# Decay rows spread by DMA into the probability tiles, and layer 1's gate scale and bias applied at its output

## The chip, the cores and the metric

One Trainium2 chip, of which the program uses one core. The metric is device time in microseconds (us). The kernel before took 1080.01 us in the median of three runs (1076.92 to 1083.23). "PE" is the matmul engine (TensorE) and "PEld" its weight loads, "DVE" is VectorE, "ACT" ScalarE, "POOL" GpSimd, "SP" SyncE, which issues nearly all DMAs.

## The reference

Forget attention, then two MLPs, all in float32 outputs (the MLP weights arrive as float64 and are split on the chip).

```python
def _attn_ref(q, k, v, s):                # q, k, v: 4 x 8 x 576 x 64; s: 4 x 8 x 576
    scale = 1.0 / np.sqrt(D)
    scores = scale * np.matmul(q, k.transpose(0, 1, 3, 2))
    cum = np.cumsum(np.maximum(s, 0.0), axis=-1)
    bias = -(cum[:, :, :, None] - cum[:, :, None, :])
    scores = np.where(causal, -1000000000.0, scores + np.minimum(bias, 0.0))
    attn = np.exp(scores - np.max(scores, axis=-1, keepdims=True))
    attn = attn / (np.sum(attn, axis=-1, keepdims=True) + 1e-09)
    return np.matmul(attn, v)

def _moe_ref(x, w_in, w_out, s, b):       # x: 2304 x 512, w_in: 512 x 2048, w_out: 2048 x 512
    r = np.maximum(x @ w_in, 0.0)
    g = s * (r * r) + b                   # s and b are one number each
    return g @ w_out

def _moe2_ref(x, w_in, w_out, alpha):
    h = x @ w_in
    g = np.maximum(h, 0.0) + alpha * np.minimum(h, 0.0)
    return g @ w_out
```

The output of the attention, heads side by side, is the input of the first MLP, and its output the input of the second.

## The kernel before, in words

**Attention.** The work is cut into 32 units (`units`): a batch, a pair of heads, and a range of rows (range 0: rows 0 to 319 in blocks 0 to 2; range 1: rows 320 to 575 in blocks 3 and 4). `sum_gates` sums the gates along the sequence, writes the sums of all 32 heads to memory (`cum_d`, L98) and turns them into a column per block (`cumT`). `load_cum` spreads one head's row of sums over all 128 partitions by a DMA whose source row is repeated (tile `cum`, L263). `scores` then makes the decay of each block on DVE: row minus column, at most 0 (L339), into the block's part of the tile `probs`; POOL clears the padding (L335) and masks the upper triangle (L343). PE's scores are added on DVE with the row maximum (L365), ACT takes the exponential (L371), POOL divides by the sum (L380). `values` turns the probabilities on PE (L411, tile `pt`) and multiplies by v (L427). A head's scores run beside the head before's values; `probs` has two buffers. Units 1 to 3 use weight slots for their tiles.

**Layer 1.** Tokens go in blocks of 256, seven of them, and one block of 512 at the end ("the wide block", `count == 2`). `up` makes `hp` (L573) in a block of 128 hidden units f; ACT applies relu and square (L586, L587), POOL multiplies by the gate's scale and adds its bias (L588), and the result is split into two parts for exact products (L106 on ACT, L107 on POOL or DVE); `down` adds to `acc` (L599) two steps later (`LAG`). `finish` takes `acc` out of PSUM, half on DVE (L614), half on ACT (L612), and the next block's first products into the same banks wait for it. The weights of f (512 KB `wi` and 512 KB `wo`) come during the first block and are converted by ACT and DVE (L116 to L118); the buffers they land in (`RAW`) are few, so a load waits for a conversion.

**Layer 2.** During layer 1's wide block `fetch` and `prepare` bring the second layer's weights in eight pairs (wi and wo of f0 into `probs` buffers, those of f1 into `xh0` and `xl0`, which are free once the last 256-token block's `up` is through), convert them, form sums (L687 to L694), split them and write them to memory (`keep`, L683). `up2` (L763) and `down2` (L845) do the products.

**Order.** The instructions are written by Python generators that alternate attention with layer 1 at a pace set by `pace`; a scheduler then puts them into one fixed order on each engine. Each engine, and SP's list of DMAs, works strictly down its list.

## Time and profile before

| | |
|---|---|
| median of three runs | 1080.01 us |
| profiled execution, its own time | 1076.26 us |
| its span, first to last instruction | 1074.5 us |
| PE, PEld busy | 94%, 86% |
| DVE, ACT, POOL busy | 70%, 60%, 53% |
| mean granted PE clock | 0.978 of full |

A busy PE is one with a matmul under way by the profiler's model. Rows of a timeline give the start in us from the span's start, the duration, the engine, the line of the program, the tiles written and read, and in brackets the idle time before it with what ended it. A group's row gives the count behind an x, then busy time and the mean of one in ns.

### The profile page before, as it was taken

The numbers are of one execution on the slowest core, as the hardware profiler recorded it, in microseconds if no ns is written. First come the engines' busy times: TensorE is split into PE (matmuls) and PEld (weight loads), VectorE is DVE, ScalarE is ACT, GpSimd is POOL, SyncE is SP. The second block draws the span as 40 slices with busy tenths as digits, with TensorE's granted clock in tenths as the row PEclk, the third lists the DMA queues.
The fourth block names the chain that finished last, engine by engine and source line by source line (L and its number), as shares of the span: only waits on it lengthen the run. The fifth ranks groups of instructions, "written<-read, shape, count | busy, mean of one in ns | idle before, by whom it ended". The sixth has DMA issues, their size and how long they took to land.

```text
span 1074.5 us, 19671 instructions
## 1 busy us (share of the span) xinstructions
PE 1010.3 (94%) x6325; PEld 922.3 (86%) x6325; DVE 750.6 (70%) x1689; ACT 644.0 (60%) x1573; POOL 566.0 (53%) x987
## 2 busy tenths in 40 slices
PE   6799979989999999999999499699999999999998
PEld 4578869979999999999998478599899899999987
DVE  7789756687667666787651487897677566865665
ACT  3778557777777777868765376566354533543342
POOL 5444458877788677988774465542235211411121
PEclk9889999999999999999999789899999999999999
DMA  6897333343233332333331679998668565585511
GB/s 145 223 276 242 80 80 64 76 96 76 40 82 77 80 74 50 88 65 77 94 90 46 226 278 341 371 368 291 205 193 265 198 205 179 160 271 186 173 43 60
DMA packets 218216, 167.41 MB, mean 156 GB/s; under 512 B 140608, under 2 KB 164672, under 8 KB 218112
## 3 DMA queue, kind: packets, MB, share of 16 engines
q1 hardware_dynamic: 216432, 165.58, 51.7%
q8 instruction: 50, 0.82, 0.3%
q10 hardware_dynamic: 1680, 0.57, 0.2%
q14 instruction: 54, 0.44, 0.1%
HBM read 133.51 MB, written 32.58 MB: 155 GB/s over the span
## 4 chain that ended last, share of the span: by engine, by line
PE 70%; DVE 9%; DMA 6%; POOL 5%; ACT 4%; issue 3%; SPq 2%; DVEq 0%; POOLq 0%; ACTq 0%
PE d L845 19%; PE u L763 16%; PE hp L573 12%; PE acc L599 12%; PE av L427 4%; PE pt L411 4%; DMA wo<-in_moe_w_out_dram 2%; POOL r L588 2%; DVE probs L339 1%; PE sc L364 1%; PE sc L363 1%; DMA wi<-in_moe_w_in_dram 1%; PE sc L361 1%; SPq L240 1%; DVE probs L365 1%
## 5 line engine op out<-in xcount | busy, mean ns | idle before, releaser
L107 POOL TENSOR_TENSOR g<-r,g 128x256 fp32r<-128x256 f32 (+1 forms) x144 | 137.4, 954 | 274.0 <-ACT g L106 273.8
L573 PE MATMUL hp<-xh,w 128*128 128x256 f32 (+1 forms) x1024 | 231.4, 303 | 5.2 <-ACT r L586 3.6
L845 PE MATMUL d<-rw,g 128*128 128x512 f32 x864 | 211.3, 392 | 0.0
L599 PE MATMUL acc<-g,w 128*128 128x256 f32 x1344 | 200.6, 288 | 3.3 <-POOL g L107 1.9
L763 PE MATMUL u<-x,rw 128*128 128x384 f32 x1008 | 193.1, 340 | 9.4 <-ACT p L776 7.4
L763 PEld LDWEIGHTS u<-x,rw 128*128 128x128 f32 x1008 | 181.7, 191 | 16.7 <-ACT p L776 7.7
L845 PEld LDWEIGHTS d<-rw,g 128*128 128x128 f32 x864 | 161.1, 188 | 30.4
L573 PEld LDWEIGHTS hp<-xh,w 128*128 128x128 f32 x1024 | 173.1, 191 | 13.3 <-ACT r L586 5.3
L599 PEld LDWEIGHTS acc<-g,w 128*128 128x128 f32 x1344 | 176.1, 190 | 8.0 <-POOL g L107 2.7
L573 PE MATMUL hp<-xl,w 128*128 128x256 f32 (+1 forms) x512 | 152.8, 298 | 0.0
L106 ACT CAST g<-r 128x256 fp32r<-128x256 f32 (+1 forms) x208 | 94.3, 454 | 64.4 <-POOL r L588 29.4
L588 POOL TENSOR_SCALAR r<-r,gate_s,gate_b 128x256 f32<-128x256 f32 (+1 forms) x128 | 96.1, 751 | 49.5 <-ACT r L587 45.1
L380 POOL TENSOR_SCALAR probs<-probs,sm 64x64 f32<-64x64 f32 (+4 forms) x160 | 93.2, 594 | 36.2 <-DVE sm L377 30.3
L371 ACT ACTIVATE probs<-probs,nm 64x64 f32<-64x64 f32 (+4 forms) x160 | 89.9, 562 | 36.9 <-DVE nm L365 36.3
L853 DVE SCALAR_TENSOR_TENSOR sum<-d,sum 128x512 f32<-128x512 f32 x126 | 86.3, 686 | 33.9 <-PE d L845 33.7
L573 PEld LDWEIGHTS hp<-xl,w 128*128 128x128 f32 x512 | 98.0, 191 | 3.2 <-issue 0.7
L798 ACT ACTIVATE r<-u 128x384 f32<-128x384 f32 x72 | 36.7, 511 | 105.0 <-PE u L763 102.8
L365 DVE CUSTOM_DVE_ANT_0 probs<-sc,probs 128x320 f32<-128x320 f32 (+3 forms) x160 | 67.8, 426 | 43.8 <-PE sc L364 35.6
L411 PE MATMUL pt<-ident,probs 128*128 128x128 f32 x480 | 78.2, 284 | 13.7 <-POOL probs L380 13.6
L800 DVE SCALAR_TENSOR_TENSOR r<-v,nalpha,r 128x384 f32<-128x384 f32 x96 | 61.5, 643 | 31.0 <-ACT v L799 30.3
L411 PEld LDWEIGHTS pt<-ident,probs 128*128 128x128 f32 x480 | 56.9, 145 | 21.1 <-POOL probs L380 15.9
L339 DVE TENSOR_SCALAR probs<-cum,cumT 64x64 f32<-64x64 f32 (+4 forms) x160 | 66.1, 462 | 11.8 <-DMA cum<-cum_d 4.7
(141 smaller groups left out, 1763.1 us busy)
## 6 DMA issues: line engine op xcount, KB each, us to landing
rw<-wq SPq DMA_DIRECT2D x231, 256.0 KB, 4.1
wi<-in_moe_w_in_dram SPq DMA_DIRECT2D x32, 512.0 KB, 5.8
wo<-in_moe_w_out_dram SPq DMA_DIRECT2D x32, 512.0 KB, 5.7
cum<-cum_d SPq DMA_DIRECT2D x32, 288.0 KB, 3.6
wq<-rw SPq DMA_DIRECT2D x33, 256.0 KB, 6.0
wq<-q_xs SPq DMA_DIRECT2D x19, 256.0 KB, 5.4
cum<-cum_d SPq DMA_DIRECT2D x30, 160.0 KB, 3.1
nat<-in_k_dram SPq DMA_DIRECT2D x64, 72.0 KB, 2.4
```

The source lines that it names most:

```text
L106: nc.scalar.copy(hi, src)
L107: lo_eng.tensor_tensor(out=lo, in0=src, in1=hi.bitcast(F32), op=ALU.subtract)
L365: nc.vector.tensor_tensor_reduce(out=pt[:rows, j0:j1], in0=scr, in1=pt[:rows, j0:j1], scale=-SCALE, scalar=init, op0=ALU.add, op1=ALU.min, ...
L371: nc.scalar.activation(pt[:rows, :n], pt[:rows, :n], AF.Exp, bias=nm[:rows, m : m + 1], scale=-1.0, accum_out=sm[:rows, m : m + 1],)
L380: nc.gpsimd.tensor_scalar(out=probs[r][:rows, :n], in0=probs[r][:rows, :n], scalar1=sm[:rows, m : m + 1], scalar2=1.0, op0=ALU.mult, op1=A ...
L411: nc.tensor.transpose(tp[:, o : o + P], u.probs[h][r][:, k0 : k0 + P], ident)
L573: nc.tensor.matmul(hs, a[:, c], b[c], start=(n == 0), stop=(n == len(terms) * NCC - 1))
L588: nc.gpsimd.tensor_scalar(out=r, in0=r, scalar1=gate_s[:, 0:1], scalar2=gate_b[:, 0:1], op0=ALU.mult, op1=ALU.add)
L599: nc.tensor.matmul(banks[d] if count == 2 else acc[:, d], a[:, d * P : (d + 1) * P], b, start=(f == 0 and (d % 2 == 0 or count == 2) and n ...
L763: nc.tensor.matmul(dst, a[:, cols], b, start=(first and terms == 0), stop=(terms == 5), skip_group_check=True)
L845: nc.tensor.matmul(bank, a[:, cols], b, start=(terms == 0), stop=(terms == 5))
L853: nc.vector.scalar_tensor_tensor(out=total, in0=bank, scalar=1.0 / W_SCALE, in1=total, op0=ALU.mult, op1=ALU.add)
```

## The change

The rows of the decay no longer pass through DVE for every block. `sum_gates` makes, for all 32 heads at once, one row per block that is already relative to the block's first column, padded with zeros, five subtractions on 32 partitions in all, and writes them to two tensors in memory (768 and 1088 columns a head). `load_bias` spreads such a row over 128 partitions straight into the tile `probs`. What a row's own sum would have subtracted is the same for the whole row and falls out in the softmax. `probs` now has three buffers, the tiles `cum` are gone; sums and temporaries of layer 2 that used `cum` use `probs` and `res`. In layer 1, relu squared goes unscaled into the products; the scale is applied when `acc` leaves PSUM, with a bias of b times the column sums of `w_out`, which POOL adds up while the weights come (`colw`) and four one-column matmuls finish. The evictions of a 256-token block become four of 256 columns.

```diff
+    WIDE = [sum(-(-i1 // P) * P if i1 < S else S for _, i1 in IB[r]) for r in (slice(0, 3), slice(3, 5))]
+    bias_d = [dram.tile([B * H, n], F32, name=f"bias{z}_d") for z, n in enumerate(WIDE)]
...
-        nc.scalar.dma_start(out=cum_d, in_=cum)
-        for r, (i0, i1) in enumerate(IB):
-            n = i1 - i0
-            tp = ps.tile([P, 512], F32, tag="b", bufs=4, name=f"tp{r}")
-            nc.tensor.transpose(tp[:n, : B * H], cum[:, i0:i1], ident[: B * H, : B * H])
-            nc.vector.tensor_copy(cumT[:n, r, :], tp[:n, : B * H])
+        for z, blocks in enumerate((IB[:3], IB[3:])):
+            rows = two.tile([B * H, WIDE[z]], F32, tag="probs", name=f"bias{z}", bufs=3)
+            nc.gpsimd.memset(rows, 0.0)
+            col = 0
+            for i0, i1 in blocks:
+                nc.vector.tensor_scalar(
+                    out=rows[:, col : col + i1], in0=cum[:, :i1], scalar1=cum[:, i0 : i0 + 1], scalar2=None,
+                    op0=ALU.subtract,
+                )
+                col += -(-i1 // P) * P if i1 < S else S
+            nc.scalar.dma_start(out=bias_d[z], in_=rows)
...
+        if f == 0:
+            nc.gpsimd.tensor_scalar(out=colw, in0=values_[1], scalar1=1.0, scalar2=0.0, op0=ALU.mult, op1=ALU.add)
+        else:
+            nc.gpsimd.tensor_tensor(out=colw, in0=colw, in1=values_[1], op=ALU.add)
+        if f == NF - 1:
...
+                nc.tensor.matmul(
+                    total[:, d : d + 1], colw[:, d * P : (d + 1) * P], onecol, start=(d == 0), stop=(d == NCC - 1),
+                    skip_group_check=True,
+                )
...
-    def load_cum(u, heads=(0, 1)):
+    def load_bias(u, heads=(0, 1)):
...
+            row = bias_d[u.rng][u.b * H + u.h0 + h]
+            if u.early:
+                spans = ((0, 384), (384, 768))
...
+                whole = two.tile([P, 1088], F32, tag="probs", name=f"probs_{u.tag}_{h}", bufs=3)
...
+                (nc.sync if u.n else nc.scalar).dma_start(out=part, in_=row[c0:c1].partition_broadcast(P))
...
-            if width > i1:
-                nc.gpsimd.memset(pt[:, i1:], 0.0)
             if r == 0:
                 nc.gpsimd.memset(pt[64:P, 0:64], 0.0)
-
-            nc.vector.tensor_scalar(
-                out=pt[:rows, :i1], in0=u.cums[h][:rows, :i1], scalar1=cumT[:rows, r, head : head + 1],
-                scalar2=0.0, op0=ALU.subtract, op1=ALU.min,
-            )
...
             nc.scalar.square(r, r)
-            nc.gpsimd.tensor_scalar(
-                out=r, in0=r, scalar1=gate_s[:, 0:1], scalar2=gate_b[:, 0:1], op0=ALU.mult, op1=ALU.add
-            )
             split(gh, gl, r, nc.gpsimd if t and count == 1 else nc.vector)
...
+                    if d % 2:
+                        nc.scalar.activation(
+                            dst, src, AF.Identity, scale=gate_s[:, 0:1], bias=bsum[:, d : d + 1]
+                        )
+                    else:
+                        nc.vector.tensor_scalar(
+                            out=dst, in0=src, scalar1=gate_s[:, 0:1], scalar2=bsum[:, d : d + 1],
+                            op0=ALU.mult, op1=ALU.add,
+                        )
...
-        a1 = whole(two, "cum", S, "a1")
+        pair = two.tile([P, 1088], U32, tag="probs", name=f"a1_{p}", bufs=3)
+        a1 = pair[:, :512]
```

The scheduler puts the whole program anew. First, PE's list where the last 256-token block ends: `acc_6` is that block's output, `hp_n` the wide block's hidden units n, and `acc_7` the wide block's output, whose first products into the old banks wait for `acc_6` to be taken out. Before:

```order
L599 MATMUL acc_6_8113<-g_15_9042,w_15_2_62_1916 128x256 x2
L599 MATMUL acc_6_8113<-g_15_9042,w_15_2_61_1917 128x256
L599 MATMUL acc_6_8113<-g_15_9042,w_15_2_62_1916 128x256
L573 MATMUL hp_8_9627<-xh_1_8800,w_8_0_32_1272 128x512
L573 MATMUL hp_8_9627<-xl_1_8801,w_8_0_32_1272 128x512
L573 MATMUL hp_8_9627<-xh_1_8800,w_8_0_31_1273 128x512
L599 MATMUL acc_7_9061<-ring_9077,w_0_2_2_177 128x512
L599 MATMUL acc_7_9061<-ring_9077,w_0_2_1_178 128x512
```

And of the changed kernel, from the same last product of `acc_6` on:

```order
L617 MATMUL acc_6_7667<-g_15_8558,w_15_2_61_1817 128x256
L617 MATMUL acc_6_7667<-g_15_8558,w_15_2_62_1816 128x256
L594 MATMUL hp_5_8955<-xh_1_8322,w_5_0_19_1052 128x512
L594 MATMUL hp_5_8955<-xh_1_8322,w_5_0_20_1051 128x512
L594 MATMUL hp_5_8955<-xl_1_8323,w_5_0_20_1051 128x512
L594 MATMUL hp_5_8955<-xh_1_8322,w_5_0_19_1052 128x512
L594 MATMUL hp_6_8985<-xh_0_8320,w_6_0_24_1091 128x512
L594 MATMUL hp_6_8985<-xl_0_8321,w_6_0_24_1091 128x512
```

Before, three matmuls of 512 columns stand between the two; now the rest of `hp_5` and all of `hp_6` to `hp_8` stand there, 40 matmuls. Both lists have done `hp_0` to `hp_8` when they come to `acc_7`. Counted from the last product of `hp_15` of the last 256-token block (after which `xh0` and `xl0` are free), 27 matmuls of 512 columns and 24 of 256 precede that place before, and 63 and 24 now.

Second, SP's list of DMAs at the end of the attention, where layer 2's weights begin (`wi_n` and `wo_n` those of f = n, `wq` the memory that `keep` writes, `x_d` layer 1's output). Before:

```order
L143 DMA wi_0_8861<-in_moe_w_in_dram 128x4x256
L147 DMA wo_0_8862<-in_moe_w_out_dram 128x1024
L683 DMA wq_102<-q_0_xs_9123 128x512
L683 DMA wq_102<-q_0_xs_9124 128x512
L143 DMA wi_2_9114<-in_moe_w_in_dram 128x4x256
L147 DMA wo_2_9115<-in_moe_w_out_dram 128x1024
L683 DMA wq_102<-q_6_xs_9128 128x512
L709 DMA x_0_1_0_9435<-x_d 128x768
L147 DMA wo_1_8866<-in_moe_w_out_dram 128x1024
L143 DMA wi_1_8865<-in_moe_w_in_dram 128x4x256
```

Of the changed kernel:

```order
L154 DMA wi_0_8382<-in_moe_w_in_dram 128x4x256
L158 DMA wo_0_8383<-in_moe_w_out_dram 128x1024
L713 DMA wq_108<-q_0_xs_8636 128x512
L713 DMA wq_108<-q_0_xs_8637 128x512
L713 DMA wq_108<-q_6_xs_8641 128x512
L739 DMA x_0_1_0_8944<-x_d 128x768
L158 DMA wo_1_8387<-in_moe_w_out_dram 128x1024
L154 DMA wi_1_8386<-in_moe_w_in_dram 128x4x256
L154 DMA wi_2_8628<-in_moe_w_in_dram 128x4x256
L158 DMA wo_2_8629<-in_moe_w_out_dram 128x1024
```

`wi_2` and `wo_2`, 1 MB, have moved from ahead of `wo_1` and `wi_1` to behind them. On DVE and ACT the evictions of `acc_6` stand, before and now, behind the conversions and splits of the first two pairs; now they stand behind the conversion of `wi_5` as well, which before came after them.

## Rows read from the trace of the kernel before

**Rows 1.** The page: busy us of each engine (share) xinstructions; GB/s in 40 equal slices.
```profile
PE 1010.3 (94%) x6325; PEld 922.3 (86%) x6325; DVE 750.6 (70%) x1689; ACT 644.0 (60%) x1573; POOL 566.0 (53%) x987
...
GB/s 145 223 276 242 80 80 64 76 96 76 40 82 77 80 74 50 88 65 77 94 90 46 226 278 341 371 368 291 205 193 265 198 205 179 160 271 186 173 43 60
```
**Rows 2.** Windows: stretch, length, busy of PE, PEld, DVE, ACT, POOL, clock, DMA share, GB/s.
```profile
0.00:160.00 160.00, 136.80 (x779) 109.04 (x779) 125.51 (x352) 103.18 (x267) 79.01 (x188) 0.96 0.65 173
160.00:560.00 400.00, 388.24 (x3165) 382.51 (x3165) 282.23 (x786) 296.84 (x799) 320.94 (x652) 1.00 0.33 73
594.70:618.70 24.00, 9.11 (x52) 7.64 (x50) 13.33 (x23) 10.10 (x19) 9.51 (x10) 0.75 0.81 266
618.70:696.60 77.90, 67.67 (x282) 55.48 (x282) 63.16 (x87) 51.28 (x95) 45.78 (x42) 0.92 0.94 329
696.60:1074.50 377.90, 373.75 (x1848) 336.82 (x1848) 260.67 (x434) 166.47 (x362) 95.54 (x78) 0.99 0.60 201
```
**Rows 3.** Windows of the start, same columns.
```profile
0.00:13.00 13.00, 4.60 (x16) 3.32 (x17) 6.60 (x23) 2.27 (x5) 7.86 (x50) 1.00 0.56 113
13.00:27.00 14.00, 12.24 (x40) 7.78 (x38) 12.55 (x52) 8.41 (x27) 8.26 (x25) 1.00 0.73 173
27.00:54.00 27.00, 21.51 (x94) 14.82 (x94) 21.48 (x74) 19.87 (x60) 11.84 (x32) 0.87 0.85 223
54.00:81.00 27.00, 25.82 (x142) 20.23 (x142) 24.00 (x56) 21.17 (x50) 11.47 (x14) 0.87 0.94 277
81.00:108.00 27.00, 25.80 (x187) 23.45 (x186) 25.62 (x56) 23.12 (x56) 12.89 (x15) 1.00 0.77 238
140.00:150.00 10.00, 7.39 (x49) 6.20 (x48) 7.71 (x24) 5.24 (x13) 5.76 (x18) 1.00 0.37 72
150.00:160.00 10.00, 7.44 (x51) 6.55 (x49) 6.19 (x21) 5.50 (x17) 5.75 (x11) 1.00 0.37 76
```
**Rows 4.** Timeline where the last 256-token block ends, all engines.
```profile
594.67 0.33 SPq L147 DMA_DIRECT2D wo<-in_moe_w_out_dram  x1
617.33 0.69 DVE L614 TENSOR_SCALAR res<-acc 128x512 f32<-128x512 f32 x1
...
618.70 2.93 PE L599 MATMUL acc<-ring,w 128*128 128x512 f32 x6 [14.89 <-ACT res L612]
```
**Rows 5.** Timeline of PE in the wide block.
```profile
666.19 2.88 PE L599 MATMUL acc<-ring,w 128*128 128x512 f32 x12
668.91 0.39 PE L573 MATMUL hp<-xh,w 128*128 128x512 f32 x1
```
**Rows 6.** The costliest groups: line, engine, operation, count, busy us, mean ns.
```profile
L588 POOL TENSOR_SCALAR r<-r,gate_s,gate_b 128x256 f32<-128x256 f32 (+1 forms) x128 | 96.1, 751 | 49.5 <-ACT r L587 45.1
L339 DVE TENSOR_SCALAR probs<-cum,cumT 64x64 f32<-64x64 f32 (+4 forms) x160 | 66.1, 462 | 11.8 <-DMA cum<-cum_d 4.7
L339 DVE TENSOR_SCALAR probs<-cum,cumT 128x576 f32<-128x576 f32 x32 | 19.9, 621 | 0.0
L339 DVE TENSOR_SCALAR probs<-cum,cumT 128x448 f32<-128x448 f32 x32 | 17.4, 543 | 2.2 <-POOL r L588 1.0 <-PE pt L411 0.8 <-issue 0.3
L107 POOL TENSOR_TENSOR vs_all<-vn,vs_all 128x512 fp32r<-128x512 f32 x12 | 15.5, 1288 | 2.3 <-ACT vs_all L106 2.2
```
**Rows 7.** DMA issues from 0 to 135 us: count, KB each, median us to landing.
```profile
cum<-cum_d SPq DMA_DIRECT2D x8, 288.0 KB, 4.1
cum<-cum_d SPq DMA_DIRECT2D x8, 160.0 KB, 3.5
```
**Rows 8.** SP's waits from 0 to 160 us: total, times, longest.
```profile
SPq L143 <- DVE wt L118: 16.9, 8, 4.0
```
**Rows 9.** The chain that ended last, at the start.
```profile
6.86 3.39 DMA cum<-cum_d
```
**Rows 10.** Timelines of PE and POOL in the middle of the attention.
```profile
245.07 0.71 PE L411 MATMUL pt<-ident,probs 128*128 128x128 f32 x5
256.63 0.63 POOL L343 TENSOR_SCALAR_AFFINE_SELECT probs<-probs 128x128 f32<-128x128 f32 x2
```

More of the change, by code (lines that the diff above doesn't have):

```diff
@@ L68, in tile_forget_attention__then__two_mlps @@
     xfp = ctx.enter_context(tc.tile_pool(name="xfp", bufs=3))
+    few = ctx.enter_context(tc.tile_pool(name="few", bufs=1))
+    small = ctx.enter_context(tc.tile_pool(name="small", bufs=2))
     dram = ctx.enter_context(tc.tile_pool(name="dram", bufs=1, space=DRAM))
@@ L72, in tile_forget_attention__then__two_mlps @@
     ps = ctx.enter_context(tc.tile_pool(name="ps", bufs=2, space=PSUM))
-    gates = two.tile([B * H, S], F32, tag="cum", name="gates")
+    gates = two.tile([B * H, S], F32, tag="probs", name="gates", bufs=3)
     nc.sync.dma_start(out=gates, in_=s.rearrange("b h t -> (b h) t"))
@@ L149, in words @@
     def words(pool, tag, name, cols=1024):
-        t = pool.tile([P, cols], U32, tag=tag, name=name)
+        t = pool.tile([P, cols], U32, tag=tag, name=name, **({"bufs": 3} if tag == "probs" else {}))
         return t[:, :1024].rearrange("p (n z) -> p n z", z=2)
@@ L166, in load_packet @@
             split(t[2 * n], t[2 * n + 1], wt)
+        if f == 0:
[3 more added lines that the diff above has]
+        if f == NF - 1:
+            total = ps.tile([P, 512], F32, tag="b", name="colsum", bufs=4)
+            for d in range(NCC):
+                nc.tensor.matmul(
+                    total[:, d : d + 1], colw[:, d * P : (d + 1) * P], onecol, start=(d == 0), stop=(d == NCC - 1),
+                    skip_group_check=True,
+                )
+            nc.vector.tensor_scalar(out=bsum, in0=total[:, :NCC], scalar1=gate_b[:, 0:1], scalar2=None, op0=ALU.mult)
         return [x.rearrange("p (c n) -> p c n", c=NCC) for x in t[:2]] + t[2:]
@@ L258, in load_v @@
             )
-    def load_cum(u, heads=(0, 1)):
+    def load_bias(u, heads=(0, 1)):
         for h in heads:
-            cr = u.buf(two, S, F32, "cum", f"cum{h}")
-            (nc.sync if u.n else nc.scalar).dma_start(
-                out=cr[:, : u.q1], in_=cum_d[u.b * H + u.h0 + h, : u.q1].partition_broadcast(P)
-            )
-            u.cums.append(cr)
+            row = bias_d[u.rng][u.b * H + u.h0 + h]
+            if u.early:
+                spans = ((0, 384), (384, 768))
+                parts = [u.buf(two, 512, F32, "", f"probs{h}{z}")[:, : c1 - c0] for z, (c0, c1) in enumerate(spans)]
+            else:
+                spans = ((0, WIDE[u.rng]),)
+                whole = two.tile([P, 1088], F32, tag="probs", name=f"probs_{u.tag}_{h}", bufs=3)
+                parts = [whole[:, : WIDE[u.rng]]]
+            for part, (c0, c1) in zip(parts, spans):
+                (nc.sync if u.n else nc.scalar).dma_start(out=part, in_=row[c0:c1].partition_broadcast(P))
+            probs, col, z = {}, 0, 0
+            for r in u.blocks:
+                width = -(-IB[r][1] // P) * P if IB[r][1] < S else S
+                if z + 1 < len(spans) and col >= spans[z + 1][0]:
+                    z += 1
+                c = col - spans[z][0]
+                probs[r] = parts[z][:, c : c + width]
+                col += width
+            u.probs[h] = probs
     def split_v(u):
@@ L316, in scores @@
         own = HALF[h]
-        head = u.b * H + u.h0 + h
         nr = len(u.blocks)
-        nm = two.tile([P, 16], F32, tag="nm", name=f"nm_{u.tag}_{h}")
-        sm = two.tile([P, 16], F32, tag="sm", name=f"sm_{u.tag}_{h}")
+        stat = small.tile([P, 8], F32, tag="stat", name=f"stat_{u.tag}_{h}")
+        nm, sm = stat[:, 0:3], stat[:, 4:7]
         if u.rng == 0:
             nc.gpsimd.memset(sm[:, 0:1], 1.0)
-        big = None if u.early else two.tile([P, 1088], F32, tag="probs", name=f"probs_{u.tag}_{h}")
-        probs, col = {}, 0
+        probs = u.probs[h]
         for r in u.blocks:
@@ L347, in scores @@
             )
-        u.probs[h] = probs
         for m, r in enumerate(u.blocks):
@@ L663, in prepare @@
         a0, a1, o0, o1 = (x.bitcast(F32) for x in (a0, a1, o0, o1))
-        s12 = whole(two, "cum", S, "s12", F32)
+        s12 = pair[:, 512:1024].bitcast(F32)
         A11, A12, A21, A22 = a0[:, :256], a0[:, 256:], a1[:, :256], a1[:, 256:]
@@ L815, in u_tile @@
         if k < 5:
-            return two.tile([P, S], F32, tag="cum", name=name)[:, :TH]
+            if not spare:
+                spare.append(one.tile([P, 1024], F32, tag="res", name="spare"))
+            return spare[0][:, (k - 3) * 512 : (k - 3) * 512 + TH]
         return one.tile([P, 10 * D], F32, tag="vn", name=name)[:, :TH]
@@ L824, in down2 @@
         if p == 0:
-            tiles = [two.tile([P, 1088], F32, tag="probs", name=f"sum{sb}_{i}") for i in range(2)]
-            tiles.append(one.tile([P, 1024], F32, tag="res", name=f"sum{sb}_2"))
+            tiles = [two.tile([P, 1088], F32, tag="probs", name=f"sum{sb}_{i}", bufs=3) for i in range(3)]
             sums[sb] = [t[:, i * 512 : (i + 1) * 512] for t in tiles for i in range(2)]
```

55 lines of the change are left out of this document (27 added, 28 removed).

## The prediction

> **What bounds the kernel now.** I read the page's busy times first, to see which engine could set the time: PE is busy for 1010.3 of 1074.5 us, and no other engine is above 750.6 [rows 1]. So whatever the change takes from DVE and POOL can only come back through the 64.2 us in which PE has nothing under way, and through stretches at a lower clock. The next view, windows cut where the kernel's stages change, says where those 64.2 us lie [rows 2]. From 160 to 560 us, attention beside layer 1's small blocks, PE is busy for 388.24 of 400 us at full clock; DVE has 118 us free there and POOL 79. From 696.60 on, layer 2, it is busy for 373.75 of 377.9. The idle time sits in two places: 23.2 us in the first 160, and 25.1 us between 594.70 and 696.60, of which 14.9 in the first 24 us.
>
> For the second place I went to the timeline [rows 4]. PE waits 14.89 us for the last 256-token block's output to be taken out of PSUM. Those two evictions wait for nothing of their own: they stand in the lists of DVE and ACT behind the conversion of layer 2's first weights, and these can be loaded (SP's row at 594.67) only when the last `up` of that block has freed its buffers. From 594.67 to the end of the wait at 618.70 is 24.0 us; PE has 9.1 us of other work for it. After that the stretch up to layer 2 is held by transfers: the DMA engines are busy for 0.94 of 77.9 us, at 329 GB/s [rows 2].
>
> For the first place the finer windows show who is full [rows 3]: from 54 to 108 us DVE is busy for 49.6 of 54 us, and the DMA engines for 0.94 and then 0.77 of the time. SP's waits say which of the two comes first: the loads of wi wait 16.9 us, in 8 pieces, for DVE's last conversion step to free a buffer [rows 8]. So the first block's weights are paced by DVE first and by the DMA engines close behind.
>
> **Removed: the decay on DVE and the gate on POOL.** 160 DVE instructions, 66.1 us, and 128 POOL instructions, 96.1 us, go [rows 6]. From 160 to 560 us nearly all of this is off PE's path, since PE has only 11.8 us there to win. A part of those waits is for probabilities that come late, and the chain behind a block loses one DVE and one POOL step; but its matmuls are issued two steps later, so most of that was hidden. I take 2 us of the 11.8, with bounds of 6 won and 5 lost (the scheduler puts all lists anew, and a list that guesses a duration wrongly can cost as well).
>
> In the first 160 us it counts for more. Units 4 to 7 have 8 heads, each with one subtraction of 448 columns and one of 576: 8 x (0.543 + 0.621) = 9.3 us of DVE time, within a stretch where DVE is the one waited for. POOL's gate was between two ACT steps of the same chain there. From 140 to 160 us PE is idle for 5.2 us [rows 3]; that is attention left over when the first block is done, and it should shorten with shorter chains: I take 2 us of it (bounds 0 and 5).
>
> **Added: bytes.** A row of range 0 grows from 160 to 384 KB, and one of range 1 from 288 to 544 KB. For units 0 to 3 that is 8 x 224 KB = 1.84 MB, for units 4 to 7 8 x 256 KB = 2.10 MB, together 3.93 MB that must pass in the first 110 us or so, beside the first layer's 16.8 MB of weights. At the 223 GB/s of 27 to 54 us the first part needs 8.2 us of DMA time; up to 54 us the DMA engines have 0.44 x 13 + 0.27 x 14 + 0.15 x 27 = 13.5 us free [rows 3]. At the 277 GB/s of 54 to 81 us the second part needs 7.6 us; from 54 to 108 they have 0.06 x 27 + 0.23 x 27 = 7.8 us free. So it fits, and just so. The most it can cost is all 8.2 + 7.6 = 15.8 us, if none of the free time lies where the bytes are wanted; the least is nothing, and DVE's 9.3 us come back whole. I take 3 us won for DVE against bytes from 54 us on, because SP's waits name DVE and not the transfers, and a third of 9.3 because the free DMA time would be used up.
>
> Before that there is the very first head. Its path was: write of the sums, spread in 3.39 us [rows 9], three subtractions on DVE. Now the three subtractions come ahead of the write (on 32 partitions; the trace has none of these, so they get the 0.46 us mean of the old ones [rows 6], which cancels them), and the spread carries 384 KB in place of 160. By the two medians, 3.5 us for 160 KB and 4.1 for 288 [rows 7], 128 KB cost 0.6 us, so 224 KB cost 1.05. I book 1 us lost. The second tensor's two subtractions come behind the first's on DVE and ahead of nothing that is urgent.
>
> After the start the bytes are no matter: 24 x 224 + 24 x 256 KB = 11.8 MB in 400 us are 29 GB/s on top of 73, with the DMA engines at 0.33 [rows 2].
>
> **Added: a wait for a buffer.** A row's DMA now needs a whole `probs` buffer, so it waits until the transposes of the head three before are done, and SP's list stands behind it (the loads of q, k and v of the next units). In the middle of the attention the transposes of one head end at 245.8 us, and the head three behind it is masked at 256.6 [rows 10]: 10.8 us, for a transfer that by the same slope takes 4.1 + 2 x 0.6 = 5.3 us for 544 KB. With 5.5 us left this wait costs nothing.
>
> **Added: the column sums and four evictions in place of two.** POOL adds 16 times 128x512; its nearest row, two inputs of that size, is 1.29 us [rows 6], so 21 us, where the gate took 16 x 0.75 = 12 of the same stretch. POOL is busy for 79 of 160 us there; the work it delays is masks. Cost nothing, and up to 5 us if a mask stands behind a sum whose weights are late. The evictions have halves of the old size; the four one-column matmuls and the five dropped transposes are below a microsecond or two on a PE that waits anyway. Nothing.
>
> **Moved: work for PE in the long wait.** By the lists, 63 matmuls of 512 columns and 24 of 256 now lie between the freeing of the buffers and the wait, in place of 27 and 24. Twelve of 512 columns take 668.91 - 666.19 = 2.72 us [rows 5], 0.227 each, so 36 more are 8.2 us. Put the other way, the buffers are freed 8.2 us of PE work earlier, and all that hangs on them follows earlier: the conversions, the evictions, the 77.9 us of transfers behind. Against it stands that `wi_2` and `wo_2`, 1.05 MB, are now loaded behind that point: at 329 GB/s 3.2 us, of which some fits into the 0.19 x 24.0 = 4.5 us that the DMA engines have free in that stretch [rows 2]; I book 2 us. The evictions behind one more conversion may come up to 3 us later. Won: 6 us, with bounds of 2 and 10. What is late next is still the same eviction, some 7 us instead of 14.9, since 24.0 less 17.3 are left.
>
> **The sum.** Against the profiled execution's 1076.3 us: -6 at the long wait, -3 from 54 to 140 us, +1 at the first head, -2 from 140 to 160, -2 from 160 to 560, nothing in layer 2, whose PE time is the same: -12, 1064.3 us. The median of the runs shown lies 3.7 us above that execution (1080.0), so 1068 us.
>
> **Rivals.** (a) DVE alone paced the start. Then the 9.3 us come back whole, the 5.2 us of idle time at 140 to 160 go, and the long wait gives its 8.2 + 2 us: 1080 - 9.3 - 5.2 - 10.2 + 1 = 1056. For it: SP's waits. Against it: 0.94 of DMA time from 54 to 81 us. (b) The scheduler's new lists give the 8.2 us back: the evictions move as far behind as PE's work moved ahead, by the extra conversion and the later weights, and the start stays as it is: 1080 to 1077. For it: the same chain of conversions holds both. Against: most of that chain is unchanged. (c) Slower: the DMA engines become the bound of the first 110 us. From the point where their free time there, 21 us, is not where the rows are wanted, each row holds back the weights queued behind it in SP's list; the price is the 15.8 us worked out above, plus 1 for the first head, less the 6 at the long wait and none of the other gains: 1080 + 16.8 - 6 = 1091, and with half of the bytes uncovered 1083. For it: 0.94 and 0.85 of DMA time at 54 to 81 and 27 to 54 us; the row transfers go out in the same list as the weights. Against: SP waits for DVE today.
>
> On (c) the Trainium skill has a rule that speaks against the change ("DMA: Bandwidth & Descriptors", section "Where 436 GB/s comes from"): transfers between memory and the chip's buffers are bound by memory at about 358 GB/s a core, and a row that is spread over 128 partitions is read 128 times. At that rate the 3.93 MB would cost, as an estimate from the page, 11.0 us of DMA time, less than my 15.8. The trace's fullest slice moves 371 GB/s, reads and writes together [rows 1], so the page's figure is at most a little low here, and my price stands.
>
> **Chances.** The forecast, 1060 to 1074: 0.47. (a), below 1060: 0.17. (b), 1074.6 to 1080: 0.15, and (c) 0.21, of which 0.04 lie below 1085.4. A difference of 0.5%, 5.4 us, is about what a measurement of this kernel can tell from none. With 1080.0 as the measure, faster is (forecast) and (a), 0.64; same is (b) and the low end of (c), 0.19; slower is the rest of (c), 0.17. Range for 8 in 10: 1053 to 1087.
>
> **What would show it.** Right: the wait for the eviction in the last block falls to 5 to 10 us; DMA share from 54 to 108 us rises above 0.9 and PE's idle time from 140 to 160 us shrinks; PE's idle time from 160 to 560 stays near 10 us. Wrong: a wait of PE for POOL's division or for a row's DMA repeated head after head in the attention (then the buffer wait counts), or the first block ending later than before (then (c)), or the eviction's wait unchanged (then (b)).

## The result, and the profile after

The changed kernel takes 1069.76 us in the median of 14 runs (1063.05 to 1074.01) against 1077.46 for the kernel before beside it: a ratio of 0.9918, interval 0.9894 to 0.9943: 7.7 us less, clear of no difference. Its profiled execution took 1073.5 us. The page's busy times answer to [rows 1]: DVE lost 52 us, POOL 104, and PE works as long as before.

```profile
PE 1014.6 (95%) x6328; PEld 924.6 (86%) x6328; DVE 698.3 (65%) x1540; ACT 647.7 (60%) x1580; POOL 462.1 (43%) x749
```

The windows answer to [rows 2, 3], with the same columns; the last three are cut at the last `up` of the last 256-token block, at the first product into the old banks, and at the first `d`. The first two cuts are those of [rows 2]; the third is not, since 696.60 there is the end of a wait and the first `d` of the kernel before comes at 705.65.

```profile
0.00:160.00 160.00, 138.05 (x726) 109.21 (x727) 123.71 (x294) 98.43 (x253) 75.23 (x143) 0.89 0.71 196
160.00:560.00 400.00, 385.17 (x3151) 378.85 (x3150) 234.55 (x695) 301.32 (x812) 237.00 (x473) 1.00 0.42 106
54.00:81.00 27.00, 24.08 (x110) 18.65 (x110) 20.09 (x43) 15.82 (x40) 12.03 (x16) 0.75 0.85 257
81.00:108.00 27.00, 26.88 (x177) 22.52 (x175) 26.60 (x54) 20.20 (x48) 12.51 (x14) 1.00 0.89 253
27.00:54.00 27.00, 23.95 (x86) 16.00 (x85) 15.86 (x57) 15.76 (x48) 13.23 (x37) 0.68 0.79 194
140.00:160.00 20.00, 20.00 (x142) 18.13 (x141) 13.99 (x38) 13.04 (x33) 9.41 (x20) 1.00 0.35 78
...
594.90:622.50 27.60, 17.30 (x89) 14.42 (x87) 17.72 (x27) 12.56 (x24) 10.16 (x12) 0.90 0.91 311
622.50:701.90 79.40, 74.12 (x319) 62.03 (x320) 61.86 (x97) 56.17 (x104) 26.77 (x25) 0.95 0.93 326
701.90:1071.70 369.80, 365.04 (x1813) 327.72 (x1811) 254.02 (x421) 161.92 (x353) 99.26 (x82) 1.00 0.59 201
```

In the first 160 us PE does 726 matmuls where it did 779. The stretch from 27 to 81 us runs at a granted clock of 0.68 and 0.75 in place of 0.87. The freed DVE is idle there and not PE. At the other end the long wait is shorter. These two rows are the timeline of SP and PE where the last 256-token block ends, and answer to [rows 4].

```profile
594.86 0.33 SPq L158 DMA_DIRECT2D wo<-in_moe_w_out_dram  x1
...
622.48 9.31 PE L617 MATMUL acc<-ring,w 128*128 128x512 f32 x30 [10.30 <-ACT res L636]
```

To see where time was won and lost, I summed for every run the work still on PE's list at a moment, at full clock. Each matmul counts as 0.444 ns a column plus 4 ns, an estimate that makes 0.231 us for 512 columns, where [rows 5] have 0.227. The kernel whose work left is larger is behind by that much, whatever its order. In us against the profiled kernel before; minus is ahead:

```
at us            54   108   160   240   400   540   640   720  1000
changed         1.7   6.9   4.8   6.2   8.8   8.3   3.7  -2.4  -2.5
changed again   1.0   2.9   2.2   2.2   4.8   3.5  -2.3  -8.5  -8.5
decay_only      1.7   3.8  -0.2  -1.3  -0.6   0.0  -3.9 -11.9 -11.9
gate_only       0.4   4.0   3.8   4.5   7.6   3.6   0.9  -8.4  -8.5
no_sums         1.8   4.0  -2.8  -8.7  -7.2  -8.2 -12.0 -21.2 -21.1
free_sums       2.5   4.8  -3.0  -8.4  -8.9 -11.5 -16.2 -24.8 -24.7
bias_in_split   0.2   3.5   1.4  -2.9  -0.8  -2.0  -4.2 -11.3 -11.2
finish_first    0.4   5.8   4.3   5.4   7.0   5.5 -12.7 -12.6 -12.4
p_buf           0.8   3.6   4.1   5.0   5.4   5.2   6.0   4.4   6.0
wide_rows       0.4   6.3   4.2   2.9   2.9   0.6  -4.6 -15.3 -15.4
more_issues     1.0   6.7   2.8   2.7   3.2   2.0  -4.2 -13.9 -13.8
rows_act        4.8  12.9   7.0  13.3  12.9  10.1   7.9  -2.0  -1.8
bias_finish     0.4   4.8   1.2  -3.8  -2.2  -3.2 -20.6 -14.1 -14.0
```

The changed kernel is behind by 8.3 us when the attention ends and gets 10.7 back between 540 and 720 us; the forecast had it 6 us ahead at the one place and 6 more won at the other. One profile is one execution, though. `p_buf` has the lists of the kernel before up to layer 2 (on DVE, ACT and POOL the order recorded is the same up to 690 us) and is 5.2 us behind it at 540, so differences of 5 us between two rows of this table need not come from a change.

### The profile page after: what moved, and what is told of

It is laid out like the page before. It is cut to its first block, busy times and chain, and to the rows that moved or that the text cites. A ratio compares the mean times of both kernels' runs of the same rounds, so it can differ in the third digit from the quotient of the medians.

```text
span 1071.7 us, 19530 instructions
## 1 busy us (share of the span) xinstructions
PE 1014.6 (95%) x6328; PEld 924.6 (86%) x6328; DVE 698.3 (65%) x1540; ACT 647.7 (60%) x1580; POOL 462.1 (43%) x749
## 4 chain that ended last, share of the span: by engine, by line
PE 67%; DMA 13%; DVE 7%; POOL 5%; issue 3%; ACT 3%; SPq 1%; POOLq 0%; DVEq 0%; ACTq 0%
PE d L876 18%; PE u L793 15%; PE hp L594 11%; PE acc L617 10%; DMA probs<-bias_d 6%; PE pt L432 4%; PE av L448 4%; DMA wi<-in_moe_w_in_dram 2%; PE sc L382 2%; POOL probs L401 2%; PE sc L385 1%; DMA wq<-q_res 1%; PE sc L384 1%; POOL probs L365 1%; DMA wq<-q_xs 1%
## 5 line engine op out<-in xcount | busy, mean ns | idle before, releaser
L118 POOL TENSOR_TENSOR g<-r,g 128x256 fp32r<-128x256 f32 (+1 forms) x144 | 133.9, 931 | 289.6 <-ACT g L117 278.0
L617 PE MATMUL acc<-g,w 128*128 128x256 f32 x1344 | 203.1, 289 | 1.7 <-POOL g L118 1.3
L793 PEld LDWEIGHTS u<-x,rw 128*128 128x128 f32 x1008 | 180.0, 189 | 13.3 <-ACT rw L117 4.7
L392 ACT ACTIVATE probs<-probs,stat 64x64 f32<-64x64 f32 (+4 forms) x160 | 89.8, 562 | 31.8 <-DVE stat L386 24.1
L401 POOL TENSOR_SCALAR probs<-probs,stat 64x64 f32<-64x64 f32 (+4 forms) x160 | 91.7, 586 | 34.4 <-DVE stat L398 24.2
L432 PE MATMUL pt<-ident,probs 128*128 128x128 f32 x480 | 81.4, 290 | 15.5 <-POOL probs L401 15.4
L828 ACT ACTIVATE r<-u 128x384 f32<-128x384 f32 x60 | 30.7, 511 | 105.5 <-PE u L793 95.8
L607 ACT ACTIVATE r<-hp 128x256 f32<-128x256 f32 (+1 forms) x128 | 51.9, 405 | 54.0 <-PE hp L594 45.3
L830 DVE SCALAR_TENSOR_TENSOR r<-v,misc,r 128x384 f32<-128x384 f32 x96 | 62.7, 654 | 30.9 <-ACT v L829 30.2
L464 DVE TENSOR_TENSOR xf<-av,xf 64x128 f32<-64x128 f32 (+3 forms) x88 | 28.0, 318 | 63.0 <-ACT xf L463 62.5
```

Source lines behind the costliest of these rows:

```text
L118: lo_eng.tensor_tensor(out=lo, in0=src, in1=hi.bitcast(F32), op=ALU.subtract)
L392: nc.scalar.activation(pt[:rows, :n], pt[:rows, :n], AF.Exp, bias=nm[:rows, m : m + 1], scale=-1.0, accum_out=sm[:rows, m : m + 1],)
L401: nc.gpsimd.tensor_scalar(out=probs[r][:rows, :n], in0=probs[r][:rows, :n], scalar1=sm[:rows, m : m + 1], scalar2=1.0, op0=ALU.mult, op1=A ...
L432: nc.tensor.transpose(tp[:, o : o + P], u.probs[h][r][:, k0 : k0 + P], ident)
L617: nc.tensor.matmul(banks[d] if count == 2 else acc[:, d], a[:, d * P : (d + 1) * P], b, start=(f == 0 and (d % 2 == 0 or count == 2) and n ...
L793: nc.tensor.matmul(dst, a[:, cols], b, start=(first and terms == 0), stop=(terms == 5), skip_group_check=True)
```

## The experiments

Each was timed in five rounds beside the kernel before; medians in us, ratio with its interval. `gate_only`, `no_sums` and `free_sums` leave out the column sums and with them the bias.

```
changed again  1065.68  0.9897 (0.9862-0.9931)   no_sums        1052.35  0.9772 (0.9751-0.9793)
decay_only     1063.67  0.9865 (0.9847-0.9883)   free_sums      1053.01  0.9776 (0.9749-0.9803)
gate_only      1063.85  0.9866 (0.9846-0.9885)   bias_in_split  1068.08  0.9906 (0.9879-0.9933)
rows_act       1073.85  0.9970 (0.9950-0.9991)   finish_first   1062.77  0.9853 (0.9823-0.9883)
p_buf          1080.53  1.0027 (1.0005-1.0049)   bias_finish    1062.90  0.9853 (0.9831-0.9875)
wide_rows      1062.20  0.9860 (0.9838-0.9881)   more_issues    1064.51  0.9882 (0.9862-0.9903)
```

**The same kernel again.**

> The changed kernel once more, unaltered, for a second profile beside the kernels of this group. Theory (the clock decides the spread): its times spread over 1063 to 1074 us as the 14 runs before did, and the profile that is shorter than 1071.7 us has PE at the lower clock level for less than the 34 us that the first profile has in its first 160 us, by about two us for each us gained. Rival (the spread has nothing to do with the clock): the low stretches are as long, and the difference lies in waits of another place.

Its profiled execution is 6.0 us shorter (1067.51). Windows of this profile for the two stretches:

```profile
54.00:81.00 27.00, 24.68 (x143) 18.76 (x143) 24.71 (x55) 20.10 (x50) 11.45 (x15) 1.00 0.98 292
...
27.00:54.00 27.00, 21.60 (x96) 15.08 (x96) 18.71 (x61) 17.24 (x54) 14.86 (x38) 0.87 0.81 199
```

With two clock levels, one half of the other, 0.68 means 17.3 of 27 us at the lower one, and 0.75 13.5 us; here it is 7.0 and 0. So 23.8 us less at half clock, four for each us gained where I expected two. The lists are the same, and of the 6.0 us between the two executions 4.0 stand at 108 us, behind the stretch in which the clock differs. Over the 20 executions on record of this kernel, time and mean granted clock go together (correlation -0.85, 5.9 us for each 0.01 of clock); over the 17 of the kernel before that ran beside the last six they do not (0.01). What sets the clock, and which of the two drives the other, was not tried. Between kernels it does not decide: `no_sums` has 0.62 from 27 to 54 us and is 8.2 ahead at 540. From here on I compare with this second profile.

**One part alone.** `decay_only` takes the gate's part back:

```diff
+            nc.gpsimd.tensor_scalar(
+                out=r, in0=r, scalar1=gate_s[:, 0:1], scalar2=gate_b[:, 0:1], op0=ALU.mult, op1=ALU.add
+            )
...
-            nc.gpsimd.tensor_tensor(out=colw, in0=colw, in1=values_[1], op=ALU.add)
...
+                if m % 2:
+                    nc.scalar.mul(res, bank, 1.0 / W_SCALE)
```

> Only the decay's part of the change: rows by DMA as in the changed kernel, but the gate's scale and bias back on POOL, no column sums, evictions as before. Theory (the rows make the start late, the gate's removal helps it little): PE's work left at 140 us is behind the kernel before by 7 to 12 us, as in the changed kernel (10.8), and the time is 1070 to 1077 us; the wait for acc_6's eviction, with 45 matmuls of 512 columns ahead of it in place of 27 and 63, is about 14.9 - 18 x 0.227 = 10.8 us. Rival (the column sums on POOL make the start late): without them PE's work left at 140 us is within 3 us of before, and the time is 1062 to 1067.

`gate_only` makes the gate's part of the change in the kernel before, without the column sums:

```diff
-            nc.gpsimd.tensor_scalar(
-                out=r, in0=r, scalar1=gate_s[:, 0:1], scalar2=gate_b[:, 0:1], op0=ALU.mult, op1=ALU.add
-            )
...
+                            dst, src, AF.Identity, scale=gate_s[:, 0:1], bias=bsum[:, d : d + 1]
```

> Only the gate's part, on the kernel before: no multiplication on POOL, the scale at the output, evictions as in the changed kernel. The column sums are left out (and with them the bias). Theory: the start is as before, PE's work left at 108 us within 3 us, the idle time at 140 to 160 us shrinks by 2 us or so; the wait for acc_6's eviction, with 44 matmuls of 512 columns ahead of it in place of 27, falls from 14.9 to about 11 us; 1069 to 1075 us. Rival (the gate's part brings the whole gain): 1062 to 1068. Rival (it brings nothing, all gain is the decay's): 1076 to 1080.

Each part alone wins 13 us. Both together won 7.7 at first and 11.1 in this group, where the intervals overlap. Neither of the two has the column sums. My theory for `decay_only` missed by 6 us and its rival, which blames these sums, met the time; the theory for `gate_only` missed and its first rival met it. Neither wins in the start or the attention beyond what two executions differ by (0.0 and 3.6 behind at 540); both win some 12 us from there to layer 2. Their long waits, by the timeline of PE in the one and the other, were forecast at 10.8 and 11:

```profile
615.77 11.28 PE L603 MATMUL acc<-ring,w 128*128 128x512 f32 x42 [12.51 <-ACT res L619]
```

```profile
620.09 9.01 PE L599 MATMUL acc<-ring,w 128*128 128x512 f32 x30 [12.47 <-ACT res L618]
```

**The column sums.** `no_sums` leaves them out, the four small matmuls too:

```diff
-            nc.gpsimd.tensor_tensor(out=colw, in0=colw, in1=values_[1], op=ALU.add)
...
```

> The changed kernel without the column sums and so without the bias: no colw on POOL, no four small matmuls. Theory (the sums wait in POOL's list for DVE's conversions and hold back masks and divisions): POOL's 17.5 us of waiting for DVE at colw go, PE's work left at 140 us is 4 us or more ahead of the changed kernel's second profile (which is 5.4 us behind before), median 1059 to 1063. Rival (the start is late by the rows alone): as the changed kernel, 1064 to 1070, and as late at 140 us.

`free_sums` keeps the additions and takes their operand away:

```diff
-            nc.gpsimd.tensor_scalar(out=colw, in0=values_[1], scalar1=1.0, scalar2=0.0, op0=ALU.mult, op1=ALU.add)
+            nc.gpsimd.memset(colw, 0.0)
...
-            nc.gpsimd.tensor_tensor(out=colw, in0=colw, in1=values_[1], op=ALU.add)
+            nc.gpsimd.tensor_tensor(out=colw, in0=colw, in1=colw, op=ALU.add)
```

> The changed kernel, its 15 additions of 128x512 on POOL kept, but colw is added to itself (it starts at zero), so that none of them waits for a conversion on DVE; the column sums, and with them the bias, are so left out. Theory (what the sums cost is the waiting: masks and divisions stand in POOL's list behind an addition that waits for DVE): 1051 to 1057, near the kernel without sums (1052.4). Rival (it is POOL's time, 15 x 1.3 to 1.7 us): 1062 to 1070, as the changed kernel.

1052.35, 7 us below my range for `no_sums`, and 1053.01: without the waiting additions the change is 13 to 17 us faster. `free_sums` has the same 15, which wait for nothing, run early (from 4 to 53 us in place of 47 to 153 in the second profile) and take 1.03 us each in place of about 1.5. The gain comes later than I expected (1.4 us at 140, 10.9 at 240). POOL's waits from 0 to 240 us in the first profile of the changed kernel (total, times, longest):

```profile
POOL probs L364 <- DMA probs<-bias_d: 32.2, 11, 6.4
POOL colw L181 <- DVE wt L129: 17.5, 8, 5.3
...
POOL colw L181 <- DVE stat L398: 4.8, 1, 4.8
POOL colw L181 <- DVE wt L128: 4.2, 1, 4.2
POOL colw L181 <- DVE stat L397: 4.0, 1, 4.0
POOL colw L181 <- DVE last L129: 1.6, 1, 1.6
```

That is 32 us in which POOL stands at an addition (29 in the second profile), with masks and divisions behind it in its list. The first row, POOL waiting for a row to land, is not what parts the kernels: `no_sums` has 32.4 there. What PE gets done meanwhile show the windows of the changed kernel's second profile, then of `no_sums`, then of `free_sums`:

```profile
108.00:160.00 52.00, 48.29 (x315) 43.11 (x314) 42.84 (x90) 36.06 (x89) 28.61 (x45) 0.93 0.49 133
160.00:240.00 80.00, 72.40 (x583) 70.17 (x582) 45.34 (x138) 58.25 (x163) 44.36 (x97) 1.00 0.44 107
```

```profile
108.00:160.00 52.00, 51.01 (x366) 46.46 (x365) 43.97 (x107) 41.48 (x107) 24.68 (x51) 1.00 0.61 162
160.00:240.00 80.00, 77.47 (x633) 75.94 (x632) 51.25 (x146) 62.28 (x167) 48.50 (x97) 1.00 0.45 110
```

```profile
108.00:160.00 52.00, 52.00 (x384) 47.86 (x382) 42.57 (x108) 40.28 (x107) 23.49 (x50) 1.00 0.61 159
160.00:240.00 80.00, 76.70 (x627) 75.19 (x625) 48.74 (x142) 61.99 (x167) 47.85 (x97) 1.00 0.44 109
...
680.00:720.00 40.00, 38.40 (x197) 34.96 (x196) 35.13 (x58) 25.10 (x55) 14.60 (x15) 1.00 1.05 404
```

PE does 101 and 113 matmuls more from 108 to 240 us.

The obvious rival is the order: the scheduler writes all lists anew, and POOL's list in `free_sums` departs from the changed kernel's at the eleventh instruction. The table speaks against it. At 240 us every profile with waiting additions is behind, by 2.2 to 13.3 us (both profiles of the changed kernel, `wide_rows`, `more_issues`, `finish_first`, `rows_act`), and every one with rows by DMA and without them is ahead, by 1.3 to 8.7, each kernel with an order of its own. The size is less sure. Kernels with waiting additions have medians from 1062.20 to 1073.85, so at least 9 of the 13 to 17 us lie outside what a new order did here; and additions that wait longest do not make the slowest kernel (37.7 us at them in `wide_rows`, the fastest of these).

Three things are not parted: the waiting itself, the additions' own time, some 22 us, among masks that are wanted, and the later freeing of the converted weights, which the additions read. On the last, the waits for an addition that the second profile lists come to 2.1 us on PE and its loads and 1.4 on SP, which speaks for POOL's list.

**The rows as the brake.** Three kernels load the start's transfers more, or move them. `rows_act` issues the rows of units 1 to 3 from ACT's queue:

```diff
-                (nc.sync if u.n else nc.scalar).dma_start(out=part, in_=row[c0:c1].partition_broadcast(P))
+                (nc.scalar if u.n < EARLY else nc.sync).dma_start(out=part, in_=row[c0:c1].partition_broadcast(P))
```

> The changed kernel, with the rows of units 1 to 3 issued from ACT's queue in place of SP's (12 issues of about 0.47 us). Theory (SP's list is what makes the start late): the loads of the third f's weights go out at 31 to 34 us in place of 38.5, PE is at the lower clock for less than 25 us of the first 160, PE's work left at 140 us is 5 us or more ahead of the changed kernel, and the median is 1062 to 1066. Rival (the bytes make it late): the same bytes pass, so PE's work left at 140 us stays within 3 us of the changed kernel and the time within its spread, 1066 to 1074.

Its time, 1073.85, is slower than the changed kernel's and the rival's number, but it answers another question than it was meant to. ACT's timeline:

```profile
8.53 13.99 ACTq L293 DMA_DIRECT2D probs<-bias_d  x13
22.55 1.28 ACT L127 ACT_TABLE_LOAD   x1 [22.55 <-DMA probs<-bias_d]
```

Thirteen issues in a row keep ACT from its first work until 22.55 us, so it says nothing on SP's list. The issues themselves take 5.3 of these 13.99 us, most of them 0.33 each. From the fifth on each begins 0.02 us after the landing of the fourth before it (the fifth at 13.22, the first landed at 13.20): the rest is waiting for rows to land. The other two leave the queue as it is. `wide_rows` moves more bytes:

```diff
-                spans = ((0, 384), (384, 768))
+                spans = ((0, 512), (256, 768))
...
```

> The changed kernel, with the rows of units 1 to 3 loaded in parts of 512 columns in place of 384: 0.79 MB more in the first 35 us, as many DMAs. Theory (bytes pace the first 40 us): at 190 GB/s they cost 4 us, the third f's weights go out 3 to 4 us later than 38.5 to 39.7, median 1070 to 1074. Rival (the number of DMAs and the waits in SP's list pace it, not the bytes): the third f's weights go out within 1 us of the changed kernel's, median 1064 to 1070.

`more_issues` cuts each part in two:

```diff
+                cut = ((c0, (c0 + c1) // 2), ((c0 + c1) // 2, c1)) if u.early else ((c0, c1),)
+                for a, b in cut:
...
```

> The changed kernel, with each row DMA of units 1 to 3 cut in two: 12 DMAs more in SP's list, the same bytes. Theory (SP's issues pace the first 40 us): 12 x 0.47 = 5.6 us more, the third f's weights go out at 44 us in place of 38.5 to 39.7, PE's work left at 54 us falls 3 us or more further behind, median 1069 to 1074. Rival (bytes pace it): third f's weights within 2 us, median 1064 to 1070.

The third f's loads go out 3 us later than in the changed kernel's two profiles (38.54 and 39.66), by SP's timeline of `wide_rows` and `more_issues`:

```profile
41.78 0.63 SPq L154 DMA_DIRECT2D wi<-in_moe_w_in_dram  x1
```

```profile
42.64 1.82 SPq L154 DMA_DIRECT2D wi<-in_moe_w_in_dram  x1
```

Yet both are no slower than the changed kernel, 1062.20 (below both of its ranges) and 1064.51 (its rival's time). So neither 0.79 MB more nor 12 issues more cost measurable time, and neither of my theories on the rows holds. Why both even lie 1 to 8 us below its medians was not tried; since the scheduler writes all lists anew for each kernel, a difference of that size can be the order's.

**The second wait.** The timeline of PE in the kernel before has another wait, which no row of mine showed:

```profile
696.63 9.18 PE L763 MATMUL u<-x,rw 128*128 128x384 f32 x36 [7.41 <-ACT p L776]
```

`p_buf` gives that `p` a free buffer, in the kernel before:

```diff
+        if k < 5 and u_turn[0] < 7:
+            return two.tile([P, 512], F32, tag="g", name=name, bufs=3)[:, :TH]
```

> The kernel before with one line added: the first two temporaries of layer 2's first product (p and u) take a free g tile in place of a cum tile, which pair 6's conversion holds. All lists are as before up to that product; ACT's copy to p then stands eight places earlier. Theory (the part of the gain behind 640 us is this buffer): nothing changes up to 680 us, the wait of PE for ACT's p, 7.4 us, falls below 2, PE's low clock behind it goes (about 2.9 us), and the median falls from 1076.8 to 1066 to 1070. Rival (the transfers bound that stretch): the wait turns into one for rw, loaded and converted no earlier, and the time stays at 1074 to 1077.

PE's waits from 630 to 760 us, in `p_buf`; before, the list is p 7.4, rw 2.0, ring 0.9:

```profile
PE u L763 <- ACT p L776: 3.2, 2, 2.3
PE u L763 <- ACT rw L106: 1.9, 1, 1.9
PE d L847 <- ACT g L106: 1.5, 1, 1.5
PE acc L599 <- ACT ring L106: 0.9, 1, 0.9
PE u L763 <- DVE rw L107: 0.8, 2, 0.5
PE u L763 <- DVE u L772: 0.7, 1, 0.7
```

The wait for `p` is 3.2 us, not below 2, and with others of 0.5 to 1.9 us the waits come to 9.0 us in place of 10.3. The time did not fall, 1080.53 against 1077.92 beside it, above the rival's range as well: the theory falls.

**The long wait.** `finish_first` prepares each pair a step later, so that the eviction comes ahead of pair 1's conversion:

```diff
-            if f in (0, 2, 4, 6, 8, 10, 13):
-                prepare(f // 2)
+            if f in (2, 4, 6, 8, 10, 12, 14):
+                prepare(f // 2 - 1)
```

> The changed kernel, with each pair of layer 2's weights prepared one step of the wide block's loop later, so that the eviction of acc_6 stands ahead of pair 1's conversion in the lists of DVE and ACT and no longer behind it. Theory (the wait counts in full): PE's wait for the eviction falls from 10.3 to 10.7 us to 5 or less, and the median from 1066 to 1070 to 1060 to 1064. Rival (the conversions and transfers of the weights bound the stretch up to layer 2): the wait falls, but PE waits as much longer for rw, and the median stays at 1064 to 1070 or rises, since the conversions begin later.

The wait is gone altogether; windows of that stretch:

```profile
594.00:640.00 46.00, 46.00 (x212) 38.34 (x211) 36.84 (x53) 29.82 (x57) 21.31 (x20) 1.00 0.89 296
640.00:700.00 60.00, 52.09 (x225) 42.82 (x223) 49.17 (x84) 41.58 (x77) 20.00 (x18) 0.94 1.02 369
```

PE gains 18.2 us from 540 to 640 and nothing after, where the second profile of the changed kernel gains 5.8 and then 6.2. So half of what the wait gave comes back as idle time behind 640, where the DMA engines are full (1.02): theory and rival are each half right. 1062.77 lies in the theory's range, beats the kernel before clearly, and lies 3 and 7 us below the changed kernel's two medians; `wide_rows` lies as far below without this step, so its gain over the changed kernel is not shown to be the step's.

**A version without sums.** `bias_in_split` adds b/s while relu squared is split, with the second part on DVE in all blocks; `bias_finish` adds the step of `finish_first`.

```diff
+            nc.scalar.activation(gh, r, AF.Identity, bias=gate_b[:, 0:1])
+            nc.vector.scalar_tensor_tensor(
+                out=gl, in0=r, scalar=gate_b[:, 0:1], in1=gh.bitcast(F32), op0=ALU.add, op1=ALU.subtract
+            )
...
```

> A whole kernel without column sums: b/s is added where relu squared is rounded into its two parts (ACT's rounding gets it as its bias, the second part is one DVE instruction, on DVE for all blocks), and the scale s stays at the output. Theory (the sums are what the change lost): as without sums, 1048 to 1056. Rival (DVE gets 112 second parts that POOL had, and becomes late with the row maxima): 1060 to 1068.

> Both: the bias in the split and the pairs prepared a step later. By the theories of the two before it, 1044 to 1050; by the rival of the second, 1050 to 1058, no better than the bias in the split alone.

1068.08: the upper end of the rival's range. Windows of `bias_in_split` and of `no_sums`, the same stretch:

```profile
240.00:560.00 320.00, 312.69 (x2569) 308.61 (x2569) 211.15 (x605) 244.38 (x635) 141.22 (x294) 1.00 0.39 100
```

```profile
240.00:560.00 320.00, 313.58 (x2560) 308.98 (x2559) 181.88 (x529) 237.95 (x636) 189.23 (x364) 1.00 0.38 100
```

PE's first wait from 108 to 560 us, in the one and the other:

```profile
PE pt L420 <- POOL probs L389: 11.4, 10, 2.3
```

```profile
PE pt L419 <- POOL probs L388: 7.9, 11, 1.8
```

48 us less on POOL and 29 more on DVE, and PE waits 3.5 us longer for divisions. That alone does not make 15 us, and the kernel before had DVE busy for longer still in [rows 2]. Nor is this the stretch: by the work left, `bias_in_split` falls 5.8 us behind `no_sums` before 240 us, 0.4 from there to 540, and 3.7 from there to 720. The cause is open, and with it why a kernel without column sums is no faster than the changed one. `bias_finish` is at 1062.90, above both of its ranges.

## Why the prediction came out

The forecast was 1068; 1069.76 was measured, inside 1053 to 1087 and faster by 0.8%. The number is right by luck. Of the 12 us forecast 7.7 came; the kernel before was measured at 1077.46 this time, 2.5 below the 1080.0 from which the forecast counts; and within the 7.7 two errors of opposite sign nearly cancel, a loss in the start and attention and a gain ahead of layer 2. Step by step, with the second profile where a size matters:

- **The long wait, -6 (bounds 2 and 10): right.** 10.30 us are left of 14.89 (10.73 in the second profile), just above the 5 to 10 foreseen. The freed work came as counted; the eviction came later, 27.6 us behind the freeing in place of 24.0, so 3.6 us went back where I booked 2.
- **The column sums, "Cost nothing, and up to 5 us if a mask stands behind a sum whose weights are late": this step failed.** The condition was named and is what happened. Its price is 10.9 us by 240 us (2.2 behind against 8.7 ahead) and 13 to 17 in the end, part of which may be the new order. I compared POOL's busy times, 21 us against 12, and did not ask how long the head of its list would wait.
- **The start and the attention, -3, +1, -2 and -2, a sum of -6 by 560 us: wrong in the kernel as changed** (8.3 and 3.5 us behind at 540 in the two profiles). Without the sums it is -8.2 and -11.5 with both parts, so the gains were there to be had; either part alone is not ahead at 540, and `bias_in_split`, which has both, is only by 2.0. PE's idle time from 140 to 160 us is gone in the first profile (20.00 of 20 us busy), but shorter chains are not needed to explain it: 85 of its matmuls there are layer 1's, where it was 39, so more was left to fill the time. From 160 to 560 us PE's idle time was to fall by 2 us and rose by 3, from 11.8 to 14.8.
- **The wait for a buffer, "this wait costs nothing": wrong, at a small price.** The sign named for it, a wait of PE for POOL's division repeated head after head, did show. From 160 to 560 us SP stands at the rows' issues until transposes free a buffer, POOL waits for the rows to land, and PE waits for POOL twice as often and long as before (its row of before is the last):

```profile
SPq L293 <- PE pt L432: 104.1, 23, 7.8
POOL probs L364 <- DMA probs<-bias_d: 52.7, 20, 3.9
PE pt L432 <- POOL probs L401: 10.2, 10, 2.9
PE pt L411 <- POOL probs L380: 4.8, 4, 2.8
```

  Whether PE's 5.4 us more are the buffer's alone was not tried; `no_sums`, with as long a wait of SP (114.2), has 7.9.
- **DMA share above 0.9 from 54 to 108 us:** 0.85 and 0.89 in the first profile, in the second 0.98 from 54 to 81. The bytes came; that they did not bind rests on `wide_rows`.
- **Nothing from the long wait to layer 2: failed, on the good side.** From 640 to 720 the kernel gained 6.1 to 6.2 us in both profiles. The prediction gave that stretch to the transfers, but 7.41 of its 10.2 us of idle PE were the wait for `p`; `p_buf` shows that the time did not come back with a free buffer alone. Why every kernel with one of the two parts wins 9 to 18 us between 540 and 720 (`p_buf` 0.8) is not settled. In code, what `decay_only` and `gate_only` share is that the wide block's output goes to `nat`, `turned`, `xs0` and `xs1` in place of `res` and `xf`; that was not tried alone, and both also have new lists.
- **Rivals.** (a) fell: the start is not faster. (b) fell: the wait shrank and the time with it. (c) fell with the time, below its 1083, and by `wide_rows` and `more_issues`. Its sign, a first block that ends later, showed in the first profile and was a poor one: the last conversion of the block's weights ends at 160.3 and 153.2 us in the two profiles, at 145.9 in `no_sums`, and at 152.9 before, but at 159.2 in `p_buf`, whose lists there are those of before. On its rule from the Trainium skill ("DMA: Bandwidth & Descriptors", "Where 436 GB/s comes from"): the page's 358 GB/s for a core does not bind here, since `free_sums` moves 404 GB/s from 680 to 720 us, reads and writes together, with one core in use; the measurement decides.

Summed in the second profile: 3.5 behind at 540, 5.8 won to 640, 6.2 to 720, together -8.5. The first profile ends at -2.5; of these 6.0 us 4.0 stand at 108 us, behind the stretch of lower clock.

## What to carry to other kernels

An instruction added to an engine that "has room" is priced by what it waits for and by what stands behind it in that engine's list, not by its busy time alone; ask of each when its operand is ready, and put it where that is long past. Where a change has two parts, run each alone, and the pair without what only the pair needs: here either gave 13 us, and both without the sums 25. Where a scheduler writes all lists anew, a few us between two kernels can be the order's; a sign that holds over several orders is worth more than one median. A wait that is taken away is worth only what the next resource lets through, so run the version that removes it wholly before counting it.

## What the runs showed of the hardware

- Two executions of one program differed by 6.0 us, and the granted clock from 27 to 81 us was 0.68 and 0.75 in one, 0.87 and 1.00 in the other; over 20 executions the time rose by 5.9 us for each 0.01 of mean granted clock less.
- Thirteen issues of row DMAs held ACT's queue for 13.99 us (`rows_act`): 5.3 us of issuing, the rest waiting, from the fifth on each until the fourth before it had landed.
- An instruction of DVE or POOL that begins while the other engine works can take longer. From the timeline of both in the kernel before:

```profile
683.63 0.68 DVE L107 TENSOR_TENSOR rw<-o,rw 128x512 fp32r<-128x512 f32 x1
683.68 1.49 POOL L719 TENSOR_TENSOR t<-x,x 128x384 f32<-128x384 f32 x1 [1.47 <-DMA wq<-q_vs]
684.23 1.49 DVE L118 SCALAR_TENSOR_TENSOR o<-wo,o 128x512 uint32<-128x512 uint32 x1
685.25 1.35 POOL L720 TENSOR_TENSOR x<-x 128x384 f32<-128x384 f32 x1
685.64 1.50 DVE L107 TENSOR_TENSOR rw<-a,rw 128x512 fp32r<-128x512 f32 x1
```

  The first DVE row begins with POOL idle and takes 0.68 us; the last, of the same operation and shape, begins inside POOL's addition at 685.25 and takes 1.50. POOL's at 683.68 begins inside a DVE row and takes 1.49. It is not the rule: of this operation and shape, 103 begin inside a POOL instruction and have a median of 0.68 and a longest of 1.51; the 57 others stay at 0.69 or less.
